# RWKV attention with a mixture of experts: the bonus term as column-half matmuls, one step order for all chunks, zero-padded tiles, four routing groups

## The chip, the cores and the metric

The kernel runs on one core of one Trainium2 chip. The metric is the device time of one execution in microseconds, as the median of three runs: 420.6 us before the change (420.49 to 426.0).

## The reference

The inputs r, k, v are 4 batches x 8 heads x 768 positions x 48, in fp32. Attention first, a linear recurrence for each batch and head, with a decay w and a bonus u for each head and channel:

```python
for t in range(S):
    cur = np.einsum('bhd,bhe->bhde', u[None] * kt, vt)
    y[:, :, t] = np.einsum('bhd,bhde->bhe', rt, state + cur)
    state = w[None, :, :, None] * state + np.einsum('bhd,bhe->bhde', kt, vt)
```

Its result, as 3072 tokens x 384, goes through a mixture of 8 experts (384 to 1024 to 384) in which each token uses one expert:

```python
e_idx = np.argmax(x @ w_gate, axis=1)
probs = softmax(x @ w_gate)                 # gate_w: probs at e_idx
eom = 1.0 / (1.0 + np.exp(-(x @ w_output_gate)))
h = np.maximum(x[mask] @ w1[e], 0.0)
out[mask] = gate_w[mask, None] * eom[mask, e, None] * (h @ w2[e])
```

The bonus part of a row of y is v times one number for each token and head, the sum over d of r·u·k.

## The kernel before

**Attention in chunks.** The 3072 tokens are 24 chunks of 128 (six to a batch), and the 8 heads four pairs, each pair on the 128 partitions as two halves of 64 rows. Rn and Kn are r and k times powers of the decay (`prep`, two VectorE products, L217); `trans` turns them into RT and KT on TensorE (L264), copied out by ScalarE (L265). `scores` (L277) multiplies KT and RT into two PSUM tiles ps_a; `causal` (L281) masks them into two tiles A on VectorE. `inter` (L315) adds the state T's share of y, `intra` (L323) the chunk's own, both in PSUM (ps_y). `state` (L293) makes the new state; VectorE adds the old one (L301) and GpSimd applies the decay (L302). The bonus: `uterm` makes ku = k·u·r by two GpSimd products (L239, L240) with u_b, a 192 KB copy of u on all partitions; `bonus` sums it over each head on VectorE (coef, L249) and multiplies v by it on GpSimd (vc, L251). `output` adds ps_y and vc on VectorE into x (L330) and stores it to x_d in DRAM (L335).

**Loads.** `load(i)` issues three DMAs of 192 KB on the sync engine's queue, in the order k, r, v (L193), into pools of four buffers each; chunks 0 to 3 have buffers of their own.

**Routing.** For each chunk, x is transposed (`logits_t`, L372, L374) and multiplied by both gates' weights, 16 columns (`logits_mm`, L382). The chunks form GROUPS; a group's `group` (L394 to L610), a generator, finds each token's expert and its place in the list of that expert, by VectorE instructions on small tiles and a few matmuls, and adds two columns (token number and weight) to a table. The table's matmul runs in bf16 with five columns: the token number in two parts, the weight in three (`parts`, `rest`, `columns`, `collect`). When all but the last group are in, the most filled expert is known and its weights are loaded; the first EARLY tiles of its tokens are gathered and its first matmuls are done during the last chunks (`early_x` L793, `early_mm`).

**The order.** All five engines run in the order in which the program is written (`manual_schedule`); nothing reorders them. For each chunk i the main loop walks through the list STEP (STEP0 for chunk 0): `sc` scores, `a0`, `a1` masks, `in` inter, `xt` transposes of x(i−1), `tr` transposes of chunk i+1, `p0`, `p1` Rn and Kn of chunk i+2, `ld` load(i+3), `bo` bonus, `i0`, `i1` intra, `st` state, `lm` logits of chunk i−1; x follows behind the list. At each `m` a few pending VectorE instructions of a group are put in, paid by the credit that BUDGETS gives from a chunk on (nominal costs in us); at each `t1` there is room for a group's matmul. So the place of a name in STEP is its place on each engine it uses, the sync engine's queue included.

After the chunks the expert phase runs: gather, transposes, three matmuls per product (the fp32 values are split in two), scale, scatter to the output.

Of the kernel before, what the change touches and what calls it, by code (L numbers as in the profile page):

```python
# [147 lines left out]
def make_powers(tc, pool, k, halfway):  # L148
# [34 lines left out]
def load_rkv(tc, pin, spare, srcs, b, c, first, after=None):  # L183
    nc = tc.nc
    ts = []
    for nm, s in zip("krv", (srcs[1], srcs[0], srcs[2])):
        if nm in first:
            t = first[nm][:, :, :D]
        elif spare:
            t = spare.pop(0).rearrange("p (h d) -> p h d", h=H)  # L190
        else:
            t = pin.tile([C, H, D], F32, name=f"{nm}_t")
        nc.sync.dma_start(t, s[b, :, c * C : (c + 1) * C, :].rearrange("h p d -> p h d"))  # L193
        ts.append(t)
        if after and nm == "k":
            after()
    return [ts[1], ts[0], ts[2]]


class Attention:  # L200
    def __init__(self, tc, ctx, k, load, x_d):
# [31 lines left out]
    def uterm(self, i):  # L233
        if i >= NT:
            return
        nc, k = self.tc.nc, self.k
        rt, kt, vt = self.load(i)
        ku = self.pw.tile([C, H, D], F32, name="ku")
        nc.gpsimd.tensor_mul(ku, kt, k.u_b.rearrange("p (h d) -> p h d", h=H))  # L239
        nc.gpsimd.tensor_mul(ku, ku, rt)  # L240
        self.ku[i] = ku

    def bonus(self, i):
        if i >= NT:
            return
        nc = self.tc.nc
        vt = self.load(i)[2]
        coef = self.pw.tile([C, H], F32, name="coef")
        nc.vector.tensor_reduce(out=coef, in_=self.ku.pop(i), axis=AX.X, op=ALU.add)  # L249
        vc = self.pw.tile([C, H, D], F32, name="vc")  # L250
        nc.gpsimd.tensor_mul(vc, vt, coef.unsqueeze(2).to_broadcast((C, H, D)))  # L251
        self.vc[i] = vc
# [86 lines left out]
class Router:  # L339
    def __init__(self, tc, pool, k, wg, wog):  # L340
        nc = tc.nc
        self.tc, self.k = tc, k
        self.wg32 = pool.tile([C, KC, 2 * E], F32, name="wg32")
        nc.sync.dma_start(self.wg32[:, :, :E], wg.rearrange("(c p) e -> p c e", p=C))
        nc.sync.dma_start(self.wg32[:, :, E:], wog.rearrange("(c p) e -> p c e", p=C))
# [31 lines left out]
    def logits_mm(self, ps, xT, tag="u"):  # L377
        pl = ps.tile([C, 512], F32, name="ps_l", tag=tag, bufs=1)
        for j in range(KC):
            for c in range(2):  # L380
# [1 line left out]
                self.tc.nc.tensor.matmul(pl[half, : 2 * E], xT[:, j, half], self.wg32[:, j, :], start=(j == 0), stop=(j == KC - 1), skip_group_check=True)  # L382
# [11 lines left out]
    def group(self, ps, w, lg, i0, G, closing, last):  # L394
# [41 lines left out]
        def weighting():  # L436
# [20 lines left out]
            rest = scale  # L457
            for i in range(3):
                nc.vector.tensor_copy(parts[:, i], rest)
                yield  # L460
                if i < 2:
                    nxt = mk(f"rest{i}")
                    nc.vector.tensor_sub(nxt, rest, parts[:, i])
                    rest = nxt
                    yield

        parts = None if last else w.tile([C, 3, G], BF16, name=f"parts_{G}", tag="parts")
# [5 lines left out]
        nc.tensor.matmul(cnt, k.tri, oh16.rearrange("p c e -> p (c e)"), start=True, stop=(G == 1 and (first or based)), skip_group_check=True)  # L473
        if not first and not based:
            nc.tensor.matmul(cnt, k.ones16, rep(self.csum16), start=False, stop=(G == 1), skip_group_check=True)
        for c in range(G - 1):
            nc.tensor.matmul(cnt[:, (c + 1) * E :], k.ones16, oh16[:, c, :].unsqueeze(1).to_broadcast((C, G - 1 - c, E)), start=False, stop=(c == G - 2), skip_group_check=True)
# [33 lines left out]
        sel = hold("sel", W, dt=BF16)  # L511
# [7 lines left out]
        ohp = hold("ohp", QP, dt=BF16)  # L519
# [3 lines left out]
        rhs = hold("rhs", 5, W, dt=BF16)  # L523
        (nc.vector if last else nc.gpsimd).tensor_mul(rhs[:, :, 0], sel, bc(k.tile0[:, cols], W))
        nc.scalar.activation(rhs[:, :, 1], sel, AF.Copy, scale=k.row1)
        tab = self.tab

        def columns(i):
            nc.vector.tensor_mul(rhs[:, :, 2 + i], sel, bc(parts[:, i], W))
# [15 lines left out]
        if last:  # L545
            yield P
            pt = product(0, 2)
            for i in range(2):
                yield V
                collect(pt, i)  # L550
# [26 lines left out]
            pt = product(2, 5)
            for i in range(2, 5):
                yield V
                collect(pt, i)  # L580
# [21 lines left out]
        collect(pt, 4)
# [13 lines left out]

    def order(self, ps, w):
# [3 lines left out]
        nc.tensor.matmul(pt[:, :E], k.ones, self.csum, start=True, stop=True)  # L621
# [782 lines left out]
```

## Time and profile before

| | |
|---|---|
| median of 3 runs | 420.6 us (420.49 to 426.0) |
| the profiled execution's own time | 422.5 us |
| its span in the profile | 420.8 us |
| TensorE busy | 372.9 us, 89% of the span |
| VectorE busy | 256.6 us, 61% |
| ScalarE busy | 152.1 us, 36% |
| GpSimd busy | 165.5 us, 39% |
| x(0), x(21), x(23) end at | 17.16, 151.46, 167.58 us |
| moved by DMA | 55.01 MB, mean 131 GB/s |

In the profile's rows PE is TensorE (PEld its weight loads), DVE VectorE, ACT ScalarE, POOL GpSimd, and SP the sync engine, SPq its DMA queue; L and a number is the line of the kernel. "out<-in" are the tiles written and read. Text in square brackets is how long the engine stood idle before the row, and what it waited for. The attention chunks fill the first 168 us of the span, the experts the rest.

### The profile page before, as it was taken

How to read it: one execution, taken by the hardware profiler on the slowest of the kernel's cores; microseconds unless marked ns; L12 is line 12 of the kernel's file. 1: busy time of each engine (PE TensorE's matmuls, PEld its weight loads, DVE VectorE, ACT ScalarE, POOL GpSimd, SP SyncE). 2: the span in 40 equal slices, each digit the busy share in tenths (PEclk: the TensorE clock that was granted, in tenths of full speed). 3: DMA queues.
4: the chain of work that ended last, by engine and by line, in shares of the span. 5: the costliest groups of instructions: out<-in, count | busy, mean ns of one | idle time of the engine just before them, and what ended most of it. 6: DMA issues, size and time to landing. Idle time of an engine off the chain costs nothing. (4 is left out here: it accounts for less than half of the span.)

```text
span 420.8 us, 11171 instructions
## 1 busy us (share of the span) xinstructions
PE 372.9 (89%) x4500; PEld 352.2 (84%) x4500; DVE 256.6 (61%) x592; ACT 152.1 (36%) x310; POOL 165.5 (39%) x215
## 2 busy tenths in 40 slices
PE   7799789878967696995998999999999999999990
PEld 4688678777867695995997999999999999999980
DVE  5878898989988963552875266266363663636300
ACT  2223232223232332421455265264453553625210
POOL 6967456555556644524041032222313503301010
PEclk8899899989979866896999999999999999999996
DMA  8957566646686611045528165174273552830010
GB/s 135 174 130 162 106 149 142 141 104 134 142 213 176 153 58 58 20 134 168 151 66 280 38 210 169 43 239 157 65 241 129 185 191 88 261 122 34 2 43 18
DMA packets 104696, 55.01 MB, mean 131 GB/s; under 512 B 78511, under 2 KB 102243, under 8 KB 104624
## 3 DMA queue, kind: packets, MB, share of 16 engines
q1 hardware_dynamic: 101200, 44.27, 41.2%
q0 software_dynamic: 3424, 9.82, 6.9%
q8 instruction: 40, 0.66, 0.6%
q14 instruction: 32, 0.26, 0.2%
HBM read 44.64 MB, written 9.76 MB: 129 GB/s over the span
## 5 line engine op out<-in xcount | busy, mean ns | idle before, releaser
L847 POOL DMA_INDIRECT out_dram<-yo,si x28 | 28.7, 1026 | 134.1 <-ACT yo L844 72.7
L810 PE MATMUL ps_h<-xh,w1h 128*128 128x384 f32 (+4 forms) x216 | 74.7, 346 | 6.0 <-issue 4.7
L811 PE MATMUL ps_h<-xl,w1h 128*128 128x384 f32 (+4 forms) x216 | 72.5, 336 | 0.0
L812 PE MATMUL ps_h<-xh,w1l 128*128 128x384 f32 (+4 forms) x216 | 72.4, 335 | 0.0
L781 POOL DMA_INDIRECT xg<-x_d,gi x28 | 31.2, 1115 | 46.0 <-PE ps_xt L793 31.1
L810 PEld LDWEIGHTS ps_h<-xh,w1h 128*128 128x128 f32 x216 | 42.6, 197 | 7.4 <-issue 5.0
L820 DVE SCALAR_TENSOR_TENSOR hl<-ps_h,hh 128x384 fp32r<-128x384 f32 (+4 forms) x72 | 38.0, 533 | 17.2 <-ACT hh L819 16.8
L819 ACT ACTIVATE hh<-ps_h 128x384 fp32r<-128x384 f32 (+4 forms) x72 | 33.7, 472 | 32.7 <-PE ps_h L812 32.7
L374 ACT COPY xT<-ps_x 128x384 f32<-128x384 f32 x24 | 11.5, 479 | 91.7 <-PE ps_x L372 83.6
L872 PE MATMUL ps_o<-w2h,hh 128*128 128x384 f32 x128 | 43.5, 340 | 0.0
L873 PE MATMUL ps_o<-w2l,hh 128*128 128x384 f32 x128 | 42.9, 335 | 0.0
L811 PEld LDWEIGHTS ps_h<-xl,w1h 128*128 128x128 f32 x216 | 42.7, 198 | 0.1
L874 PE MATMUL ps_o<-w2h,hl 128*128 128x384 f32 x128 | 42.8, 334 | 0.0
L812 PEld LDWEIGHTS ps_h<-xh,w1l 128*128 128x128 f32 x216 | 42.6, 197 | 0.2
L759 DVE TENSOR_TENSOR w1l<-raw,w1h 128x768 fp32r<-128x768 f32 x28 | 26.7, 955 | 23.4 <-ACT w1h L758 21.0
L758 ACT CAST w1h<-raw 128x768 fp32r<-128x768 f32 (+1 forms) x36 | 27.1, 764 | 27.0 <-PE ps_h L811 19.9
L281 DVE TENSOR_TENSOR A<-ps_a,mask 128x512 f32<-128x512 f32 x48 | 31.3, 683 | 5.7 <-PE ps_a L277 5.7
L796 DVE TENSOR_TENSOR xl<-ps_xt,xh 128x384 fp32r<-128x384 f32 (+4 forms) x27 | 13.9, 538 | 32.4 <-ACT xh L795 32.1
L251 POOL TENSOR_TENSOR vc<-v_t,coef 128x384 f32<-128x384 f32 x21 | 21.3, 1014 | 28.0 <-DVE coef L249 18.1
L759 DVE TENSOR_TENSOR w2l<-raw,w2h 128x768 fp32r<-128x768 f32 x28 | 26.7, 958 | 7.4 <-ACT w2h L758 5.7
L758 ACT CAST w2h<-raw 128x768 fp32r<-128x768 f32 (+1 forms) x36 | 26.7, 765 | 8.4 <-PE ps_o L874 4.4
L323 PE MATMUL ps_y<-v_t,A 128*64 128x48 f32 x672 | 29.3, 237 | 0.0
(224 smaller groups left out, 784.4 us busy)
## 6 DMA issues: line engine op xcount, KB each, us to landing
raw<-in_moe_w_dram SPq DMA_DIRECT2D x64, 384.0 KB, 3.5
x_d<-x SPq DMA_DIRECT2D x24, 192.0 KB, 1.9
v_t<-in_v_dram SPq DMA_DIRECT2D x21, 192.0 KB, 4.7
k_t<-in_k_dram SPq DMA_DIRECT2D x20, 192.0 KB, 3.0
r_t<-in_r_dram SPq DMA_DIRECT2D x20, 192.0 KB
raw<-in_v_dram SPq DMA_DIRECT2D x3, 192.0 KB
raw<-in_k_dram SPq DMA_DIRECT2D x3, 192.0 KB
xg<-x_d,gi POOLq DMA_INDIRECT x28, 4.7
```

The lines of the kernel that those rows point to most:

```text
L281: self.tc.nc.vector.tensor_mul(a, self.pa[j], self.k.mask.unsqueeze(1).to_broadcast((C, NP, C)))
L758: nc.scalar.copy(hi, self.raw[i][:, cs])
L759: (eng or nc.vector).tensor_sub(lo, self.raw[i][:, cs], hi)
L781: nc.gpsimd.indirect_dma_start(out=self.xg[q][:n], out_offset=None, in_=self.x_d[:n_x, :], in_offset=bass.IndirectOffsetOnAxis(ap=self.rt. ...
L810: nc.tensor.matmul(o, wh[:, j, fs], xh, start=(j == 0), stop=False)
L811: nc.tensor.matmul(o, wh[:, j, fs], xl, start=False, stop=False)
L812: nc.tensor.matmul(o, wl[:, j, fs], xh, start=False, stop=(j == KC - 1))
L819: nc.scalar.activation(hh, o, AF.Relu)
L820: nc.vector.scalar_tensor_tensor(hl, o, 0.0, hh, op0=ALU.max, op1=ALU.subtract)
L872: nc.tensor.matmul(o, hh, wh, start=(f == 0), stop=False)
L873: nc.tensor.matmul(o, hh, wl, start=False, stop=False)
L874: nc.tensor.matmul(o, hl, wh, start=False, stop=(f == FC - 1))
```

## The change

The bonus coefficient is made on TensorE: GpSimd multiplies RT and KT into P (`product`), eight matmuls, one for each head pair and half of the tokens, multiply P by a small matrix uw (u over the decay, zero-padded) into ps_b, and one VectorE product multiplies v by the two columns of ps_b that belong to a pair (`values`). ku, coef, the GpSimd vc and u_b go. Scores and inter use all 64 rows of a half instead of 48, and the gate weights are padded from 16 to 48 columns. STEP and STEP0 are written anew: `pr` is product, `vc` values, `x` the output, which now has its place in the list; `ld` stands behind `x`, and `p1` behind both; there are four `m` instead of six. The routing groups are four instead of five, and their table has two fp32 columns in place of five in bf16; its matmuls and the counting ones are cut into two column halves.

```diff
-GROUPS = [(0, 5), (5, 5), (10, 4), (14, 4), (18, 6)]
+GROUPS = [(0, 7), (7, 7), (14, 4), (18, 6)]
+HALVES = (slice(0, HB), slice(HB, C))
-STEP = ['m', 'sc', 'a0', 'm', 'a1', 'in', 'xt', 't1', 'm', 'tr', 't1', 'ld', 'ut', 'bo', 'm', 'p0', 'm', 'p1', 'lm', 'i0', 'st', 'i1', 'm']
+STEP = ['sc', 'a0', 'a1', 'in', 'm', 'tr', 'xt', 'p0', 'm', 'bo', 'vc', 't1', 'st', 'pr', 'i0', 'i1', 'lm', 't1', 'm', 'x', 'ld', 'p1', 'm']
-BUDGETS = [[0, 0.25], [16, 0.3]]
+BUDGETS = [[0, 0.25], [14, 0.3], [18, 0.45]]
-STEP0 = ['sc', 'a0', 'm', 'a1', 'in', 'tr', 'ld', 'bo', 'm', 'p0', 'm', 'p1', 'i0', 'st', 'i1', 'm']
+STEP0 = ['sc', 'a0', 'a1', 'tr', 'in', 'p0', 'bo', 'vc', 'st', 'pr', 'i0', 'i1', 'x', 'ld', 'p1']
...
-    def uterm(self, i):
...
-        nc.gpsimd.tensor_mul(ku, kt, k.u_b.rearrange("p (h d) -> p h d", h=H))
-        nc.gpsimd.tensor_mul(ku, ku, rt)
...
-        nc.vector.tensor_reduce(out=coef, in_=self.ku.pop(i), axis=AX.X, op=ALU.add)
-        vc = self.pw.tile([C, H, D], F32, name="vc")
-        nc.gpsimd.tensor_mul(vc, vt, coef.unsqueeze(2).to_broadcast((C, H, D)))
+    def product(self, i):
...
+        self.P = self.pw.tile([C, NP, C], F32, name="P", bufs=1)
+        self.tc.nc.gpsimd.tensor_mul(self.P, RT, KT)
+
+    def bonus(self, ps):
+        pb = self.pb = ps.tile([C, 512], F32, name="ps_b", tag="at", bufs=2)
+        for q in range(NP):
+            for half in HALVES:
+                self.tc.nc.tensor.matmul(pb[half, D * q : D * (q + 1)], self.P[:, q, half], self.k.uw[:, q, :], start=True, stop=True)
+
+    def values(self, i):
+        coef = self.pb[:, : NP * D].rearrange("p (q c) -> p q c", q=NP)[:, :, :2]
+        vc = self.pw.tile([C, H, D], F32, name="vc", bufs=1)
+        split = lambda t: t.rearrange("p (q j) d -> p q j d", j=2)
+        self.tc.nc.vector.tensor_mul(split(vc), split(self.st[i][2]), coef.unsqueeze(3).to_broadcast((C, NP, 2, D)))
...
-                rows = slice(HB * j, HB * j + D)
+                rows = HALVES[j]
...
-        self.wg32 = pool.tile([C, KC, 2 * E], F32, name="wg32")
+        self.wg32 = pool.tile([C, KC, D], F32, name="wg32")
+        nc.gpsimd.memset(self.wg32[:, :, 2 * E :], 0.0)
...
-        sel = hold("sel", W, dt=BF16)
+        sel = hold("sel", W)
-        ohp = hold("ohp", QP, dt=BF16)
+        ohp = hold("ohp", QP)
-        rhs = hold("rhs", 5, W, dt=BF16)
+        rhs = hold("rhs", 2, W)
...
             for c in range(G):
-                nc.tensor.matmul(pt[:, lo * W : hi * W], ohp[:, c, :], rhs[:, c, lo:hi].rearrange("p a w -> p (a w)"), start=(c == 0), stop=(c == G - 1), skip_group_check=True)
+                for hf in HALVES:
+                    nc.tensor.matmul(pt[hf, lo * W : hi * W], ohp[:, c, hf], rhs[:, c, lo:hi].rearrange("p a w -> p (a w)"), start=(c == 0), stop=(c == G - 1), skip_group_check=True)
...
-        load(1, lambda: nc.sync.dma_start(u_b, u.rearrange("h d -> (h d)").unsqueeze(0).to_broadcast((C, DM))))
+        k.ut = load_heads(tc, const, u, "ut", 0.0)
+        load(1)
...
+                        elif a == "x":
+                            X[i] = att.output(i)
...
-                    x = att.output(i)
```

The change moves rows on three engines at places that matter below. First the sync engine's queue at the end of chunks 0 and 1, before and then after; raw_71, xg_110 and the first v_t are the buffers of k, r and v of chunk 3, the k_t, r_t and next v_t those of chunk 4.

```order
18 L193 DMA raw_71<-in_k_dram 128x8x48
19 L193 DMA xg_110<-in_r_dram 128x8x48
20 L193 DMA v_t<-in_v_dram 128x8x48
21 L335 DMA x_d<-x 128x384
22 L193 DMA k_t<-in_k_dram 128x8x48
23 L193 DMA r_t<-in_r_dram 128x8x48
24 L193 DMA v_t<-in_v_dram 128x8x48
25 L335 DMA x_d<-x 128x384
```

```order
18 L339 DMA x_d<-x 128x384
19 L200 DMA raw_71<-in_k_dram 128x8x48
20 L200 DMA xg_110<-in_r_dram 128x8x48
21 L200 DMA v_t<-in_v_dram 128x8x48
22 L339 DMA x_d<-x 128x384
23 L200 DMA k_t<-in_k_dram 128x8x48
24 L200 DMA r_t<-in_r_dram 128x8x48
25 L200 DMA v_t<-in_v_dram 128x8x48
```

Each chunk's loads have moved behind the store of one more x: those of chunk 3 stood ahead of the store of x(0) and now stand behind it, and so on to the last chunk.

Then VectorE in chunk 2, before and after; the second number of a name counts its buffers, A is the masked score tile, and the r_t and k_t that it reads here are those of chunk 4.

```order
46 L281 TENSOR_TENSOR A_561<-ps_a_543,mask 128x512
47 L281 TENSOR_TENSOR A_563<-ps_a_544,mask 128x512
48 L249 TENSOR_REDUCE coef<-ku 128x8
49 L217 TENSOR_TENSOR Rn_297<-r_t,PR 128x8x48
50 L217 TENSOR_TENSOR Kn_300<-k_t,PK 128x8x48
51 L301 TENSOR_TENSOR T_643<-ps_u,T 128x192
52 L330 TENSOR_TENSOR x<-ps_y,vc 128x384
```

```order
47 L285 TENSOR_TENSOR A_572<-ps_a_554,mask 128x512
48 L285 TENSOR_TENSOR A_574<-ps_a_555,mask 128x512
49 L222 TENSOR_TENSOR Rn_304<-r_t,PR 128x8x48
50 L255 TENSOR_TENSOR vc<-raw_71,ps_b 128x384
51 L305 TENSOR_TENSOR T_635<-ps_u,T 128x192
52 L334 TENSOR_TENSOR x<-ps_y,vc 128x384
53 L222 TENSOR_TENSOR Kn_307<-k_t,PK 128x8x48
```

The reduction has gone, the product vc stands behind Rn and ahead of T and x, and Kn has moved behind x. The r_t that Rn reads here was issued two stores of x earlier before, and one store earlier now.

Last TensorE, the second half of chunk 1 and the first scores of chunk 2, before and after; ps_y is the output, ps_u the state's update, ps_t the transposes, ps_x the transposed x of chunk 0, ps_l its logits, ps_b the bonus columns. "64x128" and "128x128" are a matmul's output.

```order
45 L315 MATMUL ps_y<-T,RT 64x48 x16
46 L372 MATMUL ps_x<-ident,x 128x128 x3
47 L264 MATMUL ps_t<-ident,Kn_301 128x128 x4
48 L264 MATMUL ps_t<-ident,Rn_297 128x128 x4
49 L382 MATMUL ps_l<-wg_151,xT 64x16 x6
50 L323 MATMUL ps_y<-raw_69,A_446 64x48 x8
51 L293 MATMUL ps_u<-raw_69,Kn_300 64x48 x8
52 L323 MATMUL ps_y<-raw_69,A_448 64x48 x8
53 L277 MATMUL ps_a_543<-RT,KT 64x128 x2
```

```order
46 L319 MATMUL ps_y<-T,RT 64x48 x16
47 L268 MATMUL ps_t<-ident,Kn_308 128x128 x4
48 L268 MATMUL ps_t<-ident,Rn_304 128x128 x4
49 L377 MATMUL ps_x<-ident,x 128x128 x3
50 L249 MATMUL ps_b<-uw,P 64x48 x8
51 L297 MATMUL ps_u<-raw_69,Kn_307 64x48 x8
52 L327 MATMUL ps_y<-raw_69,A_451 64x48 x8
53 L327 MATMUL ps_y<-raw_69,A_453 64x48 x8
54 L387 MATMUL ps_l<-wg_153,xT 64x48 x6
55 L281 MATMUL ps_a_554<-RT,KT 64x128 x2
```

The bonus matmuls have come in, the transposes of x stand behind those of Kn and Rn, the state ahead of intra and the logits at the end. In both orders the form changes three times in a chunk: 48-row inputs (scores, inter) to full 128x128 transposes to 64-row outputs and back.

More of the change, by code (lines that the diff above doesn't have):

```diff
@@ L171, in make_powers @@
     k.pr, k.pk, k.w128 = pr, pk, sq[7]
+    k.uw = pool.tile([C, NP, D], F32, name="uw")
+    nc.gpsimd.memset(k.uw, 0.0)
+    for j in range(2):
+        rows = slice(HB * j, HB * (j + 1))
+        nc.gpsimd.tensor_mul(k.uw[rows, :, j], k.ut[rows], sq[0][rows])
 def make_tables(tc, pspool, k):
@@ L180, in make_tables, with load_rkv @@
         nc.scalar.copy(dst, ps[:, :, :D])
-def load_rkv(tc, pin, spare, srcs, b, c, first, after=None):
+def load_rkv(tc, pin, spare, srcs, b, c, first):
     nc = tc.nc
@@ L456, in weighting @@
             yield
[L457 to L467, printed above, removed]
         side = iter(()) if last else weighting()
@@ L472, in group @@
         based = last
[L473 to L477, printed above, removed]
+        halves = (slice(0, C),) if last else HALVES
+        for hf in halves:
+            nc.tensor.matmul(cnt[hf], k.tri[:, hf], oh16.rearrange("p c e -> p (c e)"), start=True, stop=(G == 1 and (first or based)), skip_group_check=True)
+            if not first and not based:
+                nc.tensor.matmul(cnt[hf], k.ones16[:, hf], rep(self.csum16), start=False, stop=(G == 1), skip_group_check=True)
+            for c in range(G - 1):
+                nc.tensor.matmul(cnt[hf, (c + 1) * E :], k.ones16[:, hf], oh16[:, c, :].unsqueeze(1).to_broadcast((C, G - 1 - c, E)), start=False, stop=(c == G - 2), skip_group_check=True)
         next(side, None)
@@ L522, in group, with weights @@
         yield Slot(0.3)
-        rhs = hold("rhs", 5, W, dt=BF16)
-        (nc.vector if last else nc.gpsimd).tensor_mul(rhs[:, :, 0], sel, bc(k.tile0[:, cols], W))
-        nc.scalar.activation(rhs[:, :, 1], sel, AF.Copy, scale=k.row1)
+        rhs = hold("rhs", 2, W)
+        (nc.vector if last else nc.gpsimd).tensor_mul(rhs[:, :, 0], sel, bc(k.id1[:, cols], W))
         tab = self.tab
-        def columns(i):
-            nc.vector.tensor_mul(rhs[:, :, 2 + i], sel, bc(parts[:, i], W))
+        def weights():
+            nc.vector.tensor_mul(rhs[:, :, 1], sel, bc(self.scale[:, cols], W))
         def product(lo, hi):
@@ L546, in group @@
             yield P
[L547 to L550, printed above, removed]
+            pt = product(0, 1)
+            yield V
+            collect(pt, 0)
             yield V
@@ L569, in group @@
             yield SPLIT
-            parts = w.tile([C, 3, G], BF16, name=f"parts_{G}", tag="parts")
             for _ in weighting():
                 yield V
-            for i in range(3):
-                columns(i)
-                yield V
+            weights()
             yield P
[L577 to L580, printed above, removed]
+            pt = product(1, 2)
+            yield V
+            collect(pt, 1)
             yield V
@@ L589, in group @@
             yield V
-        for i in range(3):
-            yield Slot(0.2)
-            columns(i)
+        yield Slot(0.2)
+        weights()
         yield P
-        pt = product(0, 5)
+        pt = product(0, 2)
         if closing:
-            self.early(pt[:, 5 * W :])
-        for a, b in ((0, 2), (1, 3)):
+            self.early(pt[:, 2 * W :])
+        for a in range(2):
             yield V
             collect(pt, a)
-            collect(pt, b)
-        yield V
-        collect(pt, 4)
         if closing:
@@ L620, in order @@
         pt = ps.tile([C, 512], F32, name="ps_ord", tag="g", bufs=1)
-        nc.tensor.matmul(pt[:, :E], k.ones, self.csum, start=True, stop=True)
+        for hf in HALVES:
+            nc.tensor.matmul(pt[hf, :E], k.ones[:, hf], self.csum, start=True, stop=True)
         yield V
@@ L1159, in rwkv_top1_moe, with load @@
         ready, pin = {}, []
-        def load(i, after=None):
+        def load(i):
             if i < NT and i not in ready:
-                ready[i] = load_rkv(tc, pin and pin[0], spare, (r, kk, v), *divmod(i, NCH), k.raw0 if i == 0 else {}, after)
+                ready[i] = load_rkv(tc, pin and pin[0], spare, (r, kk, v), *divmod(i, NCH), k.raw0 if i == 0 else {})
             return ready.get(i)
@@ L1278, in rwkv_top1_moe @@
                     att.prep(*a)
[L1279 to L1281 removed]
+                att.product(0)
+                X = {}
                 for i in range(NT):
```

80 lines of the change are left out of this document (32 added, 48 removed).

## The prediction, made before the changed kernel ran

> **What bounds the kernel now.** I read the busy times by stage first. x(n) is the attention output of chunk n, and its VectorE row (L330) marks the chunk's end. The rows shown run from the end of x(0) (17.16) to those of x(21) and x(23), to the steady expert phase and to the end. A row gives the stretch, its length, busy time (and instructions) of PE, PEld, DVE, ACT and POOL, granted clock, DMA share and GB/s.
>
> ```profile
> 17.16:151.46 134.30, 112.71 (x2708) 102.31 (x2712) 117.03 (x292) 40.23 (x104) 81.77 (x91) 0.91 0.63 142
> 151.46:167.58 16.12, 12.86 (x254) 11.30 (x246) 7.91 (x25) 4.07 (x11) 7.03 (x8) 0.71 0.24 75
> 167.58:196.00 28.42, 23.54 (x168) 22.71 (x169) 12.21 (x50) 8.31 (x23) 12.34 (x13) 0.86 0.32 100
> 196.00:420.80 224.80, 211.98 (x1235) 207.74 (x1233) 107.86 (x189) 95.75 (x166) 51.23 (x48) 0.98 0.41 130
> ```
>
> After 196 us TensorE is busy 94% of the time with expert matmuls that the change leaves alone. The 134.30 us from x(0) to x(21) are what it works on: 21 chunks, 6.4 us each, TensorE busy 84%, VectorE 87%. So neither alone sets the pace. A chunk without routing-group work shows which does when it is undisturbed (timeline: start, duration, engine, line):
>
> ```profile
> 63.92 1.10 PE L277 MATMUL ps_a<-RT,KT 48*64 48x128 f32 x32
> 65.81 0.55 PE L372 MATMUL ps_x<-ident,x 128*128 128x128 f32 x3 [0.33 <-DVE A L281]
> 67.16 0.53 PE L382 MATMUL ps_l<-wg,xT 128*64 128x16 f32 x12
> 67.53 0.65 PE L323 MATMUL ps_y<-v_t,A 128*64 128x48 f32 x16
> 68.03 0.67 PE L293 MATMUL ps_u<-v_t,Kn 128*64 128x48 f32 x16
> 68.53 0.64 PE L323 MATMUL ps_y<-v_t,A 128*64 128x48 f32 x16
> 69.10 0.89 PE L277 MATMUL ps_a<-RT,KT 48*64 48x128 f32 x24
> 64.04 0.56 DVE L330 TENSOR_TENSOR x<-ps_y,vc 128x384 f32<-128x384 f32 x1
> 65.06 1.29 DVE L281 TENSOR_TENSOR A<-ps_a,mask 128x512 f32<-128x512 f32 x2 [0.46 <-PE ps_a L277]
> 66.27 0.54 DVE L249 TENSOR_REDUCE coef<-ku 128x8 f32<-128x384 f32 x1
> 66.73 0.55 DVE L217 TENSOR_TENSOR Rn<-r_t,PR 128x384 f32<-128x384 f32 x1
> 67.19 1.18 DVE L217 TENSOR_TENSOR Kn<-k_t,PK 128x384 f32<-128x384 f32 x1
> 68.82 0.36 DVE L301 TENSOR_TENSOR T<-ps_u,T 128x192 f32<-128x192 f32 x1 [0.45 <-PE ps_u L293]
> 69.22 0.56 DVE L330 TENSOR_TENSOR x<-ps_y,vc 128x384 f32<-128x384 f32 x1
> ```
>
> Scores start at 63.92 and again at 69.10: 5.18 us, TensorE-bound but for its wait of 0.33 on the mask. 21 such chunks are 109 us; the other 25 of the 134 are what the routing groups push in, mostly on VectorE.
>
> **Where the next loads stand.** This decides the forecast. The sync queue in the same chunk, the landing of its k load (last line of the loads' answer, 64 to 71 us), and what DMA moved (the last column is GB/s):
>
> ```profile
> 64.63 0.36 SPq L335 DMA_DIRECT2D x_d<-x  x1
> 65.04 0.42 SPq L193 DMA_DIRECT2D k_t<-in_k_dram  x1
> 65.50 0.70 SPq L193 DMA_DIRECT2D r_t<-in_r_dram  x1
> 66.32 0.54 SPq L193 DMA_DIRECT2D v_t<-in_v_dram  x1
> DMA to landing us min/median/max: 3.2/3.2/3.2
> 66.20:67.20 1.00, 1.00 (x12) 0.83 (x10) 1.00 (x4) 0.75 (x2) 0.74 (x2) 1.00 0.92 177
> 67.20:68.20 1.00, 1.00 (x35) 1.00 (x34) 1.00 (x2) 0.78 (x3) 0.76 (x1) 1.00 0.97 195
> 68.20:69.20 1.00, 1.00 (x36) 0.95 (x38) 0.54 (x2) 0.00 (x0) 0.00 (x0) 1.00 1.05 209
> 69.20:69.80 0.60, 0.60 (x24) 0.60 (x28) 0.56 (x1) 0.00 (x0) 0.54 (x2) 1.00 0.20 53
> ```
>
> The queue runs in order, so k, r and v leave behind the store of x: x ends at 64.60, k is issued at 65.04, r at 65.50. k lands 3.2 us after its issue, at 68.24. Then r: the three loads of 192 KB end by about 69.4, at some 195 GB/s or 1 us apiece. I put r 0.8 us behind k, at 69.04, which is **4.4 us after x ends**. The bounds are 3.6 (together with k) and 4.8 (with the last byte). Before, the loads behind x(n) are for chunk n+4 and nothing on TensorE or VectorE waits for them. After, they are for chunk n+3, and their first user, the Rn product of chunk n+3, is a VectorE row of chunk n+1, between its mask products and its vc, T and x. A stall there holds all three, and x(n+1) releases the next loads.
>
> On this the Trainium skill, page "DMA: Bandwidth & Descriptors", section "Rules for kernel authors", says to issue a transfer early and wait on it late. The change does the reverse; by that rule alone the chunk grows by whatever latency is not covered. The trace agrees insofar as only GpSimd shows a wait for these loads before.
>
> **The new loop, x(n) to x(n+1).** Landing of r 4.4; Rn to the next row 0.46 (66.73 to 67.19); vc the same 0.46, since it is a 128x384 product out of PSUM like x (0.56 busy); T 0.36; x 0.56. Sum 6.24 us, against 5.18 for TensorE. The loop repeats 21 times: 131.0. In three of them (last chunk of a batch) T is absent, −1.1: **129.9**.
>
> **The edits by part.** The coefficient reduction (0.54) goes and the product vc (0.56) comes on VectorE: nothing. GpSimd loses ku and its vc and gains P:
>
> ```profile
> L251 POOL TENSOR_TENSOR vc<-v_t,coef 128x384 f32<-128x384 f32 x21 | 21.3, 1014 | 28.0 <-DVE coef L249 18.1
> ```
>
> Three such instructions of 1.0 us become one of 512 elements, by size 1.35; it starts when the transposes are copied and is wanted a chunk later, so it is hidden, and if it weren't it would cost at most its 1.35 per chunk. TensorE gains the bonus matmuls, 16 records in 128x64 like those of L323 (67.53 to 68.03): 0.50. Its chunk, without the wait for the mask, becomes 4.85 + 0.50 = 5.35 at most, inside the loop. Wider logits cost nothing: 12 records of width 16 took 0.37 (67.16 to 67.53), 16 of width 48 took 0.50, both 31 ns each. 64 rows in place of 48 are one record each as before. If the loop didn't cover TensorE, these would cost 0.5 per chunk.
>
> The mode order hides nothing large either. The step from the last L323 to the scores took 0.57 where the one within the mode took 0.50: 0.07 per change of mode, three per chunk before and, counted in the order, three after. The Trainium skill ("TensorEngine Tiling (Array Packing)", "Key Properties") says a mode change drains the array; with half the group matmuls freed of such changes the sum would fall by under 2 us, and TensorE waits in that time anyway.
>
> **Routing work inside the loop.** VectorE groups by line, 17.2 to 151.4 us (count | busy us, mean ns):
>
> ```profile
> L281 DVE TENSOR_TENSOR A<-ps_a,mask 128x512 f32<-128x512 f32 x42 | 27.4, 682 | 4.0 <-PE ps_a L277 4.0
> L217 DVE TENSOR_TENSOR Kn<-k_t,PK 128x384 f32<-128x384 f32 x20 | 17.3, 864 | 0.0
> L217 DVE TENSOR_TENSOR Rn<-r_t,PR 128x384 f32<-128x384 f32 x20 | 13.3, 663 | 0.0
> L330 DVE TENSOR_TENSOR x<-ps_y,vc 128x384 f32<-128x384 f32 x21 | 11.6, 550 | 1.3 <-PE ps_y L323 0.6 <-POOL w1l L759 0.6
> L249 DVE TENSOR_REDUCE coef<-ku 128x8 f32<-128x384 f32 x21 | 11.4, 543 | 0.0
> L529 DVE TENSOR_TENSOR rhs<-sel,parts 128x160 bf16<-128x160 bf16 (+1 forms) x12 | 6.7, 571 | 0.0
> L301 DVE TENSOR_TENSOR T<-ps_u,T 128x192 f32<-128x192 f32 x15 | 5.3, 354 | 7.3 <-PE ps_u L293 6.4 <-PE ps_y L323 0.9
> L459 DVE CAST parts<-rest 128x5 bf16<-128x5 f32 (+1 forms) x8 | 4.6, 576 | 0.0
> ```
>
> The six rows of chunk work are 86 of the 117 us, so about 30 are group work. It loses the parts (4.6, and some 2 in smaller rows), two thirds of the rhs columns (4.5), one of five groups and most collects (3); wider fp32 tiles give back an estimated 1. About 16 stay. Of the four places for it in a chunk, two (behind the masks, behind Kn) lie in the wait for r or before the scores, two (behind Rn, behind T) in the loop: half, **8 us**, between 5 and 10. The first expert's weights join the queue around chunks 18 to 20 (by the order, one to three at a time behind a chunk's loads):
>
> ```profile
> raw<-in_moe_w_dram SPq DMA_DIRECT2D x64, 384.0 KB, 3.5
> ```
>
> Two take 4 us at 195 GB/s, behind v's end at 4.8, so the last reaches some 2.5 us into the next loop of 6.24 and delays its r by an estimated 1 us, in two chunks: **+2**, between 0 and 4. That gives 129.9 + 8 + 2 = 140 against 134.3: **+5.7**.
>
> **The two ends.** At the start VectorE waits for GpSimd's ku; at the end TensorE waits for the gathered rows and then runs slowly:
>
> ```profile
> 13.99 0.55 DVE L249 TENSOR_REDUCE coef<-ku 128x8 f32<-128x384 f32 x1 [0.82 <-POOL ku L240]
> 163.21 1.83 PE L793 MATMUL ps_xt<-ident,xg 128*128 128x128 f32 x6 [2.97 <-DMA xg<-x_d,gi]
> 161.50:171.70 10.20, 8.46 (x70) 7.81 (x71) 1.83 (x4) 4.71 (x12) 5.27 (x6) 0.50 0.13 42
> ```
>
> Without ku, chunk 0 saves that wait, one reduction and the moved Kn, **−2** (0 to −2.5). Chunks 22 and 23 load nothing that is waited for: two TensorE chunks and a little, 10.7 instead of 16.1, if the closing group's indices come in time, **−5.4** (0 to −6). Then the half clock (0.50) on the first expert matmuls goes as well, of 4.1 us behind 167.58 about half: **−2**; wider last tables **+0.5**.
>
> **Sum.** 5.7 − 2 − 5.4 − 2 + 0.5 = −3.2 us. The profiled execution took 422.5 us by its own time, with a span of 420.8 us; 419.3 by that. The median of the three runs is 420.6, so 417.4 by that: I say **418**, no change that counts.
>
> **Rivals.** (A) *r comes in time.* If it lands under 3.5 us after x, the loop is under 5.35 and TensorE bounds the chunk: 21 × 5.35 = 112 us, with half of the 25 us of group stalls left some 124, so 16 less than my 140: **402**. For it: the lower bound 3.6 lies close. Against: k alone took 3.6 from x's end, and r is issued behind it. 20%. (B) *The loop is longer, and the end is slower.* One mechanism: r lands with the last byte or queues behind other traffic. Each 0.1 us is 2.1 us of time; from 4.95 us on the kernel is over 2% slower, and at 5.05 it takes 418 + 13.7 = **432**. For it: the transfers already run at 0.9 to 1.05 of the DMA engines. Against: before, the last byte of the same loads comes 4.8 us after x. 16%. (C) *The clock drops.* TensorE now idles about 1 us a chunk (6.24 − 5.35). At half clock a chunk's 5.35 us become 10.7 against 6.24, and 21 of them add 94 us: 512. The trace shows 0.50 behind a wait of 2.97 us, not behind waits below 1. 2%. The Trainium skill ("TensorE: Matmul & The Clock Gate", "What's actually happening") puts the drop behind an idle window of about 3.4 us, which fits that row; gaps of 1 us would keep the clock. (D) *The change doesn't do what it says at the end:* the closing indices come late as before, +5: **423**, inside no change; 10%, taken out of the forecast's 62% in all.
>
> **Chances.** Forecast and D 62%, A 20%, B 16%, C 2%. About 2%, 8.4 us, is what a measurement of this kernel can tell from no change. A and a slice of the forecast (r at 4.1 or less) are faster: 0.25; B and C slower: 0.18; 0.57 remain. Of the unknowns r's landing weighs most: 3.75 to 5.0 us in place of 4.4 give 404 to 431, which takes in the bounds of the smaller terms and leaves out C and half each of A and B.
>
> **What would show it.** Right: VectorE waits before Rn for r's DMA in nearly each chunk, about 1 us; x follows x in 6.2 us in chunks without group work; TensorE waits about 1 us per chunk, its clock near 1; the wait for xg at the end is gone. Wrong: the Rn row without a wait and 5.3 us per chunk (A), or 6.8 and more (B); vc or P late on TensorE's or GpSimd's account, for which I leave nothing.

## The result, and the profile after

The changed kernel takes **439.7 us** (438.5 to 440.8) against 423.3 for the kernel before over the same runs: a ratio of 1.038 (95% interval 1.028 to 1.049), slower. The forecast was no change at 418, with a range of 404 to 431. Times are medians of all runs, and ratios leave out the runs that were over 1.5% longer than the fastest of their kernel. The profiled execution took 438.5 us, its span is 436.6.

Busy times by stage of the changed kernel, cut at the ends of x(0), x(6), x(18), x(21) and x(23); the columns are those of the table shown of before:

```profile
16.22:56.29 40.07, 32.33 (x841) 29.82 (x834) 21.71 (x42) 9.60 (x23) 10.44 (x10) 0.96 0.56 120
56.29:145.13 88.84, 71.98 (x1819) 65.62 (x1814) 54.01 (x136) 20.67 (x54) 20.43 (x21) 0.94 0.54 118
145.13:173.89 28.76, 21.74 (x509) 19.20 (x509) 24.03 (x61) 8.75 (x22) 13.96 (x14) 0.88 0.61 153
173.89:184.08 10.19, 9.72 (x256) 8.92 (x257) 6.97 (x18) 4.21 (x12) 7.80 (x8) 1.00 0.41 119
184.08:436.60 252.52, 234.24 (x1435) 228.60 (x1433) 118.88 (x228) 103.41 (x187) 63.42 (x60) 0.97 0.40 127
```

From x(0) to x(21) it takes 157.67 us, where the kernel before took 134.30: 23.4 more, though VectorE is now busy for 100 of these us instead of 117. Something is waited for, and the first row shows it free of routing work: chunks 1 to 6 hold none, and still take 40.07 / 6 = 6.68 us each, with TensorE busy 81% and VectorE 54%. The list of waits names it (total us, times, longest):

```profile
DVE Rn L222 <- DMA r_t<-in_r_dram: 38.9, 18, 2.9
```

One chunk without routing work, from x(11) to x(12):

```profile
94.20 0.55 DVE L334 TENSOR_TENSOR x<-ps_y,vc 128x384 f32<-128x384 f32 x1
...
94.78 0.36 SPq L339 DMA_DIRECT2D x_d<-x  x1
95.13 1.29 DVE L285 TENSOR_TENSOR A<-ps_a,mask 128x512 f32<-128x512 f32 x2
...
95.67 0.69 SPq L200 DMA_DIRECT2D r_t<-in_r_dram  x1
...
99.22 0.56 DVE L222 TENSOR_TENSOR Rn<-r_t,PR 128x384 f32<-128x384 f32 x1 [2.80 <-DMA r_t<-in_r_dram]
99.70 0.55 DVE L255 TENSOR_TENSOR vc<-v_t,ps_b 128x384 f32<-128x384 f32 x1
100.16 0.35 DVE L302 TENSOR_TENSOR T<-ps_u,sq 128x192 f32<-128x192 f32 x1
100.43 0.55 DVE L334 TENSOR_TENSOR x<-ps_y,vc 128x384 f32<-128x384 f32 x1
100.66 0.56 PE L387 MATMUL ps_l<-wg,xT 128*64 128x48 f32 x12 [1.96 <-DVE T L302]
...
101.00 0.36 SPq L339 DMA_DIRECT2D x_d<-x  x1
```

This is the loop of the forecast: x ends at 94.75, its store and behind it r are issued, Rn starts 4.47 us after x, and vc, T and x follow. TensorE waits as well: its logits stand behind T (they use the PSUM tile that T reads), the next scores behind vc (which reads ps_b, and ps_b and ps_a share their two buffers). The chunk takes 6.22 us; 6.24 was forecast. So the mechanism was foreseen and its price in this chunk is right. What was wrong is how far this chunk speaks for the others.

### The profile page after: what moved, and what is told of

Same layout as the page of the kernel before. It is cut to its first block, busy times and chain, and to the rows that moved or that the text cites. A ratio compares the mean times of both kernels' runs of the same rounds, so it can differ in the third digit from the quotient of the medians.

```text
span 436.6 us, 12118 instructions
## 1 busy us (share of the span) xinstructions
PE 383.4 (88%) x4996; PEld 362.1 (83%) x4996; DVE 235.9 (54%) x516; ACT 150.3 (34%) x303; POOL 125.4 (29%) x170
## 3 DMA queue, kind: packets, MB, share of 16 engines
q1 hardware_dynamic: 101472, 44.08, 38.9%
## 5 line engine op out<-in xcount | busy, mean ns | idle before, releaser
L799 PE MATMUL ps_h<-xh,w1h 128*128 128x384 f32 (+4 forms) x216 | 73.4, 340 | 4.1 <-issue 4.1
L800 PE MATMUL ps_h<-xl,w1h 128*128 128x384 f32 (+4 forms) x216 | 71.5, 331 | 0.0
L770 POOL DMA_INDIRECT xg<-x_d,gi x28 | 31.2, 1116 | 45.0 <-PE ps_xt L782 29.5
L800 PEld LDWEIGHTS ps_h<-xl,w1h 128*128 128x128 f32 x216 | 41.6, 192 | 0.1
L801 PEld LDWEIGHTS ps_h<-xh,w1l 128*128 128x128 f32 x216 | 41.4, 192 | 0.2
L243 POOL TENSOR_TENSOR P<-RT,KT 128x512 f32<-128x512 f32 x24 | 32.6, 1360 | 23.1 <-ACT xT L379 17.7
L747 ACT CAST w1h<-raw 128x768 fp32r<-128x768 f32 (+1 forms) x36 | 27.1, 763 | 26.6 <-PE ps_h L800 22.9
L306 POOL TENSOR_TENSOR T<-T,sq 128x192 f32<-128x192 f32 x16 | 8.1, 506 | 87.2 <-DVE T L305 82.1
L281 PE MATMUL ps_a<-RT,KT 64*64 64x128 f32 x768 | 31.1, 299 | 2.0 <-DVE vc L255 2.0
L222 DVE TENSOR_TENSOR Rn<-r_t,PR 128x384 f32<-128x384 f32 x20 | 11.7, 587 | 38.9 <-DMA r_t<-in_r_dram 38.9
L269 ACT COPY KT<-ps_t 128x512 f32<-128x512 f32 x23 | 13.5, 586 | 54.3 <-PE ps_t L268 54.3
L387 PE MATMUL ps_l<-wg,xT 128*64 128x48 f32 x288 | 13.2, 225 | 20.4 <-DVE T L305 9.5
```

What stands on the lines that cost most here:

```text
L243: self.tc.nc.gpsimd.tensor_mul(self.P, RT, KT)
L281: nc.tensor.matmul(self.pa[j][half, q, :], KT[rows, q, half], RT[rows, q, :], start=True, stop=True)
L770: nc.gpsimd.indirect_dma_start(out=self.xg[q][:n], out_offset=None, in_=self.x_d[:n_x, :], in_offset=bass.IndirectOffsetOnAxis(ap=self.rt. ...
L799: nc.tensor.matmul(o, wh[:, j, fs], xh, start=(j == 0), stop=False)
L800: nc.tensor.matmul(o, wh[:, j, fs], xl, start=False, stop=False)
L801: nc.tensor.matmul(o, wl[:, j, fs], xh, start=False, stop=(j == KC - 1))
```

## The experiments

Each number beside a time is the ratio to the kernel before, run beside it, with its interval; the changed kernel has 1.038.

**1. The loads issued a store earlier.** In the changed kernel:

```diff
-STEP = ['sc', 'a0', ... 'm', 'x', 'ld', 'p1', 'm']
+STEP = ['ld', 'sc', 'a0', ... 'm', 'x', 'p1', 'm']
```

and the same in STEP0.

> The changed kernel with 'ld' at the head of STEP and STEP0 instead of behind 'x': the loads of chunk n+4 again leave right behind the store of x(n), as before the change, and nothing else moves. Theory L (late loads): the changed kernel's chunk is the loop store of x, landing of r, Rn, vc, T, x. Then VectorE's wait before Rn for r (38.9 us in 18 chunks) goes to nearly nothing, chunks without group work fall from 6.0-7.3 to 5.3-5.6 us, x(0) to x(21) from 157.7 to 125-138 us, and the time from 439.7 to 410-420 us. Rival S (the new step order itself, VectorE or TensorE): the wait only covers other waits; it is replaced by waits on TensorE or the masks, chunks stay over 6 us, and the time stays at 432 or more.

Measured: **409.0 us**, 0.971 (0.963 to 0.980). The waits list has no row of Rn for r any more. By stage:

```profile
15.95:47.20 31.25, 30.68 (x855) 28.43 (x850) 24.37 (x43) 9.77 (x24) 9.51 (x10) 1.00 0.71 154
47.20:116.72 69.52, 65.22 (x1810) 59.75 (x1798) 55.72 (x135) 20.26 (x52) 19.84 (x21) 1.00 0.67 146
116.72:143.19 26.47, 20.64 (x509) 18.04 (x509) 23.52 (x60) 8.68 (x22) 13.34 (x14) 0.94 0.60 160
```

Chunks 1 to 6 take 5.21 us, TensorE busy 98%; from x(0) to x(21) it is 127.24 us, 30.4 less than in the changed kernel. Rival S said that something else would be waited for and nothing much would come: it falls. Moving one name in a list turns 4% slower into 3% faster.

**2. The same lateness put into the kernel before.** There 'ld' is taken out of the two lists and load(i + 3) and load_raw stand behind att.output(i); all else is as before.

> The kernel before with its loads issued behind x instead of in the middle of the list, so that they leave one store of x later, and nothing else changed. Theory L: the same loop appears in it: r lands 4.4 to 5.2 us after x, then Rn, Kn, T, x (1.9 us): 6.3 to 7.1 us a chunk where it was 5.2, less where group work already held VectorE; 11 to 21 chunks lose 1 to 1.5 us each: 434 to 446 us, with VectorE waiting for r's DMA in most chunks. Rival S: loads a store later are still hidden by the six slots' order; at most 4 us slower, 421 to 425.

Measured: **459.3 us**, 1.093 (1.084 to 1.102), slower than theory L expected. Its waits, one chunk's rows, and the stage from x(0) to x(21):

```profile
POOL ku L239 <- DMA k_t<-in_k_dram: 76.1, 20, 5.4
DVE Rn L217 <- DMA r_t<-in_r_dram: 41.7, 18, 4.1
```

```profile
38.01 0.54 DVE L330 TENSOR_TENSOR x<-ps_y,vc 128x384 f32<-128x384 f32 x1
...
42.05 1.00 POOL L239 TENSOR_TENSOR ku<-k_t,u_b 128x384 f32<-128x384 f32 x1 [3.07 <-DMA k_t<-in_k_dram]
43.18 0.56 DVE L217 TENSOR_TENSOR Rn<-r_t,PR 128x384 f32<-128x384 f32 x1 [2.97 <-DMA r_t<-in_r_dram]
43.66 1.35 DVE L217 TENSOR_TENSOR Kn<-k_t,PK 128x384 f32<-128x384 f32 x1
44.93 0.34 DVE L301 TENSOR_TENSOR T<-ps_u,T 128x192 f32<-128x192 f32 x1
45.20 0.54 DVE L330 TENSOR_TENSOR x<-ps_y,vc 128x384 f32<-128x384 f32 x1
```

```profile
17.11:188.03 170.92, 132.10 (x2728) 118.29 (x2728) 119.04 (x292) 42.28 (x104) 84.82 (x90) 0.79 0.51 115
```

The loop appears here too, and longer: Kn stands in it, and since GpSimd's ku waits for the same loads the two run together, and Kn takes 1.35 us beside it. This chunk takes 7.19 us; a chunk of before without routing work took 5.2. Unforeseen was the clock in the last row: 0.79 over the stage where it was 0.91 before. So the 9% are the longer loop and a slower TensorE, in shares that this run doesn't separate.

**3. Only r issued first.** In load_rkv the order of the three DMAs is r, k, v from chunk 3 on.

> The changed kernel with each chunk's three loads from chunk 3 on issued in the order r, k, v instead of k, r, v: r leaves 0.46 us earlier and is the first to land. Theory L: r lands 0.5 to 1.0 us earlier, each of the 18 chunks that wait for it is shorter by as much: 9 to 18 us, 422 to 431. Rival S: no change, 437 to 442.

Measured: **423.9 us**, 1.005 (0.999 to 1.011). r lands 3.9 us after x on the mean of chunks 1 to 18, 0.84 earlier than in the changed kernel; the time falls by 15.8 us, and of VectorE's wait 12.0 us are gone:

```profile
DVE Rn L224 <- DMA r_t<-in_r_dram: 26.9, 18, 2.4
```

From x(0) to x(21) it takes 142.35 us, 15.3 less than the changed kernel: each tenth of a microsecond of r's delay is worth 1.8 us (15.3 / 8.4) there; the forecast's rival B put 2.1 on it.

**4. The loads late, but Rn behind x.** 'p0' goes from behind 'xt' to behind 'p1', the loads stay where the change put them.

> The changed kernel with 'p0' (Rn of the chunk after next) moved behind 'x' and 'p1'; the loads stay behind x. Rn then has r for over a chunk and holds no vc, T and x. Theory L: the wait for r goes as in e1 although the loads are late; Rn and Kn stand together before the masks, 0.5 us on VectorE that TensorE's scores mostly cover: 5.4 to 5.9 us a chunk, 412 to 424 us. Rival S: 432 or more.

Measured: **414.7 us**, 0.983 (0.976 to 0.990). The loads leave as late as in the changed kernel, and still nothing waits for r. It isn't the late issue alone that costs, but a late issue with its user ahead of the next release.

**5 to 8, from experiment 1 on.** What else of the change counts, with the loads early.

> The changed kernel with its loads at the head of the list (as in e1_loads_first, 409.0 us) and the five routing groups of before in place of four; the new table and list stay. Theory G (fewer groups save their fixed cost): a group is some 25 small VectorE rows of 0.15 to 0.7 us, half of them between Rn and x; one more costs 3 to 6 us: 411 to 416. Rival: group rows lie in VectorE's waits for TensorE, and five are as good as four: 407 to 411.

412.2 us, 0.980 (0.975 to 0.986): 3 us more than with four groups, inside what theory G expected, but the interval overlaps that of experiment 1; inconclusive.

> As e1_loads_first, with the padding undone: gate weights of 16 columns, and 48 rows in place of 64 in scores and inter. By the prediction's step padding costs and gains nothing (31 ns a record at both widths): 407 to 411. Rival: uniform 64-row tiles let TensorE go from scores and inter to the next form faster, so that undoing them costs 0.1 to 0.3 us in each of 24 chunks: 411 to 416.

407.3 us, 0.968 (0.964 to 0.972): the padding costs and gains nothing that can be told.

> As e1_loads_first, with 'p1' (Kn) moved from behind 'x' to right behind 'p0' (Rn). In e1, Kn behind x runs beside GpSimd's P and takes 1.18 to 1.66 us instead of 0.55, and the masks of the next chunk wait for it (they start 1.1 us after x instead of 0.4 to 0.8), while behind Rn VectorE waits 0.4 to 0.7 us for the bonus matmuls. Theory K: Kn is on e1's path in some 14 chunks with 0.3 us each: 403 to 407. Rival: TensorE bounds e1's chunk, and nothing comes of it: 408 to 411.

408.6 us, 0.972 (0.967 to 0.976): nothing. Theory K falls, and the rival's forecast holds, that TensorE (busy 98% of chunks 1 to 6 in experiment 1) is the bound.

> As e7_kn_beside_rn, with the first expert's weight splits of chunks 18 to 23 (two subtractions a chunk, 2.1 to 2.3 us on GpSimd) made on VectorE instead. In e1 chunks 19, 20 and 21 take 7.7, 10.3 and 8.5 us, and small VectorE rows that take 0.2 us elsewhere take 0.7 to 1.1 beside these subtractions. Theory C (contention of GpSimd with VectorE): without it the three chunks fall by 3 to 6 us in sum, less about 1 us of VectorE time a chunk: 1 to 4 us faster than e7. Rival: TensorE, at a lower clock there (0.83), sets these chunks, and VectorE's extra work makes them longer: 0 to 4 us slower than e7.

406.9 us, 0.970 (0.964 to 0.976), not to be told from experiment 7; chunks 19 to 21 take 26.6 us together, against 25.4 in experiment 7 and 26.5 in experiment 1. The contention itself is there. One small row of chunk 20, experiment 7 first, where GpSimd makes a split beside it, then this one, where GpSimd is idle:

```profile
132.81 0.95 DVE L457 SCALAR_TENSOR_TENSOR den<-en,se 128x4 f32<-128x4 f32 x1
```

```profile
134.06 0.15 DVE L457 SCALAR_TENSOR_TENSOR den<-en,se 128x4 f32<-128x4 f32 x1
```

VectorE is busy for 23.40 us of these chunks in experiment 7 and for 22.47 here, 3.32 of them with the splits: its other rows have lost 4.25 us, and the chunks are no shorter. So VectorE's busy time alone doesn't set them. What TensorE waits for there is seen in the changed kernel itself, in chunk 19:

```profile
146.85 1.88 DVE L517 TENSOR_TENSOR ohp<-pp,ip 128x896 f32<-128x896 f32 x1
148.65 1.27 DVE L285 TENSOR_TENSOR A<-ps_a,mask 128x512 f32<-128x512 f32 x2
149.38 0.90 PE L377 MATMUL ps_x<-ident,x 128*128 128x128 f32 x3 [2.49 <-DVE A L285]
151.35 0.56 DVE L255 TENSOR_TENSOR vc<-v_t,ps_b 128x384 f32<-128x384 f32 x1 [0.66 <-PE ps_b L249]
153.33 0.36 DVE L305 TENSOR_TENSOR T<-ps_u,T 128x192 f32<-128x192 f32 x1 [1.42 <-PE ps_u L297]
```

Routing rows at the place behind Kn push the masks to 3.5 us after x (145.13), TensorE waits for them, and then VectorE's vc and T wait for what TensorE makes behind them.

**9. Routing rows moved into the wait.** In the changed kernel, with the loads late, the two places between Rn and x go ahead of Rn:

```diff
-... 'tr', 'xt', 'p0', 'm', 'bo', 'vc', 't1', 'st', 'pr', 'i0', 'i1', 'lm', 't1', 'm', 'x', ...
+... 'tr', 'xt', 'm', 'm', 'p0', 'bo', 'vc', 't1', 'st', 'pr', 'i0', 'i1', 'lm', 't1', 'x', ...
```

> The changed kernel, its loads still behind x, with the two places for routing-group rows that lie between Rn and x moved ahead of Rn, into VectorE's wait for r. The prediction's step: group rows between Rn and x lengthen the loop, rows ahead of Rn are hidden in the wait. In the changed kernel chunks 7 to 18 take 85 us against 78 at the pace of chunks 1 to 6, and chunk 7, 14 and 18 also wait there 0.9 us for the logits. If the step holds, 5 to 9 us go: 430 to 435. Rival: the group rows then delay Rn itself or the masks by as much: 437 to 442.

Measured: **432.7 us**, 1.019 (1.011 to 1.026), its interval just clear of that of the 1.038: some 8 us less by the ratios (0.020 x 420.6), with the ends of the two intervals 1 to 16. (Chunks 7 to 18 of the changed kernel take 88.84 us, not the 85 of the expectation.) Routing rows between Rn and x lengthen the loop, as the prediction's step has it.

**10. The bonus as before, the rest of the change kept.** In the kernel of experiment 1 the matmuls of bonus are left out, product makes ku and values makes coef and vc, each a chunk earlier than in the changed kernel: the VectorE reduction and the three GpSimd products are back.

> As e1_loads_first (409.0), with the bonus made as before the change: ku in two GpSimd products, coef as a VectorE reduction, vc as a GpSimd product, u_b loaded; list, groups, table and padding stay. By the prediction's step the bonus alone is worth nothing on VectorE (0.54 for 0.56) and costs TensorE 0.5 a chunk, and GpSimd's 3.6 us a chunk would be hidden: where TensorE bounds e1's chunk this kernel is up to 0.5 us x 13 chunks = 6 us faster: 402 to 409. Rival B: GpSimd's three products slow VectorE's Rn and Kn and hold the start (ku): 3 to 10 us slower, 412 to 419.

Measured: **404.8 us**, 0.954 (0.948 to 0.959), clear of experiment 1. With the loads early TensorE bounds the chunk and the bonus matmuls stand in it. The starts of the scores of two chunks in a row, from x(12) on, show by how much, experiment 1 first, then this one:

```profile
81.27 1.10 PE L281 MATMUL ps_a<-RT,KT 64*64 64x128 f32 x32
84.10 0.67 PE L249 MATMUL ps_b<-uw,P 128*64 128x48 f32 x16
86.45 0.78 PE L281 MATMUL ps_a<-RT,KT 64*64 64x128 f32 x20
```

```profile
79.82 1.10 PE L280 MATMUL ps_a<-RT,KT 64*64 64x128 f32 x32
84.54 0.67 PE L280 MATMUL ps_a<-RT,KT 64*64 64x128 f32 x16
```

5.18 against 4.72 us: 0.46 us, the 0.5 of the forecast. This is the fastest version of all. The matmul bonus costs; what is left of the change here, the order with early loads, the four groups, the table and the padding, is together 4.6% faster than the kernel before. Of these only the groups and the padding were taken back alone (experiments 5 and 6); order and table were not told apart.

**11 and 12, towards a better order.**

> As e7_kn_beside_rn (408.6: loads at the head, Kn behind Rn), with the place for group rows ahead of x moved up to behind vc, so that no group row waits for the chunk's logits ahead of x. In e7 chunks 7, 14 and 18 take 6.5 to 6.7 us, 1.2 to 1.5 more than the clean ones. If that wait is the cause, 3 to 4 us go: 404 to 406. Rival: the time moves to the next chunk's masks: 407 to 410.

409.7 us, 0.967 (0.960 to 0.974): nothing; the rival's time holds. In the profiled run, the longest of the four, chunks 7, 14 and 18 do fall, to 5.2, 5.2 and 5.4 us, but chunks 19 to 21 take 31.3 us where experiment 7 has 25.4: the work has moved there.

> As e11, with 0.38 instead of 0.45 of credit for group rows at each place from chunk 18 on. In e1 and e7 chunks 19 to 21 take 25 to 27 us against 15 to 16 for clean ones, the masks start 2 to 3.5 us after x because group rows stand ahead of them, and TensorE waits up to 2.5 us for the masks. If it is the rows ahead of the masks, fewer of them a chunk spread the same work: 1 to 3 us faster than e11. Rival: all of that work has to be done before the early gather anyway, and it only moves to chunk 22: within 1 us of e11, or slower if the gather comes late.

409.8 us, 0.965 (0.958 to 0.971): within 1 us of experiment 11; the rival's time holds here too, and chunks 19 to 21 take 29.5 us. That the routing work has to be somewhere ahead of the early gather is the rival's reason; nothing here tests it by itself.

## Why the prediction was wrong

**The loop: right.** Late loads, Rn behind them, vc, T and x behind Rn. Experiments 1 to 4 show it from four sides: the wait goes when the loads leave earlier or when Rn stands elsewhere, it comes when the loads of the kernel before are made late, and it scales with r's place in the queue. Only the sign that I gave for it was too small: the waits before Rn are 2.2 us on average (38.9 / 18), where I wrote about 1.

**The landing of r: mis-sized, the first step that failed.** I took 4.4 us from one chunk, and gave 4.8, the last byte in that same chunk, as its upper bound. Over chunks 1 to 18 of the changed kernel r lands 4.14 to 5.46 us after x, on average 4.75. In nine of them it is 4.1 to 4.8 (mean 4.4, as forecast), in the other nine 4.5 to 5.5 (mean 5.1). What goes with the two sorts is told in the last section. Behind the landing the chain took 1.76 us, not 1.84. The loop is so 6.5 us, and 21 of them are 136.7 against my 129.9, some 7 us more; about 1 of it is the T that I took off in three chunks, where the chain still took 1.67 us or more. That 4.4 suits nine chunks is luck of the chunk I chose: a single chunk's row gave a value but no bounds. That landings spread could be read in the kernel before, in the same answer on the loads for the whole span, where k's landing goes to 4.7, and I quoted the one chunk instead:

```profile
DMA to landing us min/median/max: 2.7/3.0/4.7
```

**Routing work in the loop: mis-sized, the second step that failed.** I put 8 us on it and 2 on the weights' traffic. Chunks 7 to 18 take 88.84 us against 12 x 6.5 = 78, 11 more, and chunks 19 to 21 take 28.76 against 19.5, 9 more: 20 us. The weights' 2 are not seen: in chunks 19 to 21 r lands 4.3 to 5.1 us after x, as elsewhere. Nearly all of the 20 lies behind Rn. About 12 us are routing rows that stand between Rn and x, 5 of them in chunks 19 to 21. About 7 are VectorE's waits between Rn and x, for TensorE or for the logits that ScalarE copies from it; for these I had left nothing. So 12 and 7 stand where the forecast has 8, and experiment 9 gains some 8 by moving the rows.

**"Two places lie in the wait": right for Rn, not for TensorE.** Rows ahead of Rn hardly delay Rn itself, which starts 4.65 to 5.12 us after x even in chunks 19 to 21. But in chunks 19 and 20 so many of them stand ahead of the masks that these start 3.5 us after x; the wait for r is gone there (in chunk 21 it is 1.05 us), and VectorE waits 3.4 us in the two chunks for TensorE, which runs late behind the masks. Chunk 20 shows both kinds, the wait and then ten routing rows between T and x:

```profile
162.06 0.36 DVE L305 TENSOR_TENSOR T<-ps_u,T 128x192 f32<-128x192 f32 x1 [0.50 <-PE ps_u L297]
...
163.04 1.23 DVE L439 TENSOR_SCALAR eidx<-m 128x4 f32<-128x4 f32 x1
...
164.55 0.54 DVE L334 TENSOR_TENSOR x<-ps_y,vc 128x384 f32<-128x384 f32 x1
```

How much of the 9 us of these three chunks belongs to the rows' number, how much to their slowness beside GpSimd and how much to TensorE's clock (0.82 and 0.83 in chunks 19 and 20) stays open.

**The sum, term by term.** From x(0) to x(21) +23.4 where I had +5.7. The start −0.9 (x(0) ends at 16.22 instead of 17.16; forecast −2). From x(21) to x(23) 10.19 instead of 16.12, −5.9 (forecast −5.4): the gather is in time, rival D was not needed, and the clock there is 1.00. Behind it −0.7 (forecast −1.5). The total, +15.8, is the difference of the two spans.

**The rivals.** B, the longer loop, had the right side, with its point of 4.95 us; r's mean of 4.75 alone would have stayed within 2%, and the routing work did the rest. That these two errors add on the same side was not in the range, which moved r alone. C came in small part: the granted clock is 0.94 to 0.96 up to x(18) and 0.88 in chunks 19 to 21. I had read half clock off one wait of 2.97 us; the last section shows it beside waits of 1.7 to 2.4. A's chunk came true as soon as the loads were early (5.21 us for its 5.35).

**The edits at no cost.** The padding cost nothing that could be told (experiment 6). GpSimd's products and VectorE's exchange of coef for vc weren't tried alone; with all of the old bonus back, experiment 10 is faster. That the bonus matmuls were free only under the cover of the loop, and cost 0.5 us a chunk without it, is what experiment 10 shows.

## What to carry to other kernels

When a transfer is issued behind the result of a step, ask which step its first user stands in and whether that user is ahead of the next release: if so, issue, landing and the chain behind them are a loop, and its sum, not any engine's busy time, is the pace. The size of such a loop needs the spread of the landing over many steps, since its price is multiplied by all of them. An edit that is free under a wait should be priced again without that wait before it is kept.

## What the runs showed of the hardware

The two sorts of chunks differ by one small transfer. From x(10) on (end 87.62) the changed kernel's DMA shows this; the first two rows are tenths of busy time and GB/s in 40 slices of 87.6 to 93 us, then the instruction queue (packets, MB, share), two of the issues (us to landing), and the issue of r on the sync engine's queue (start, duration):

```profile
DMA  0000002999854679999721000000396799999677
GB/s 0 0 0 0 0 0 80 440 341 216 262 168 84 107 134 176 230 229 203 142 46 17 11 11 11 23 20 17 84 151 119 159 235 253 253 238 191 124 122 146
q8 instruction: 1, 0.02, 2.0%
x_d<-x SPq DMA_DIRECT2D x1, 192.0 KB, 4.0
r_t<-in_r_dram SPq DMA_DIRECT2D x1, 192.0 KB, 4.5
88.53 2.21 SPq L200 DMA_DIRECT2D r_t<-in_r_dram  x1
```

One packet of 16 KB on an instruction queue starts at 88.59 and takes 1.71 us. Then, from about 90.4 to 91.4, traffic falls to 11 to 23 GB/s, with one packet at a time in flight; only then does the store of x land, after 4.0 us, and the traffic rises again with k and r. From x(11) on, without such a packet between x and r's landing, the store lands after 2.0 us, r 3.5 us after its issue, and the issue itself takes 0.69 us instead of 2.21:

```profile
x_d<-x SPq DMA_DIRECT2D x1, 192.0 KB, 2.0
r_t<-in_r_dram SPq DMA_DIRECT2D x1, 192.0 KB, 3.5
```

Over the 18 chunks the trace has such a packet start within 3 us behind x in just the nine with the mean of 5.1. The split comes back in two other traces: in experiment 3, r lands 4.5 us after x on average in the eight chunks with such a packet and 3.5 in the other ten; in experiment 2, 5.3 in five and 4.6 in thirteen. My reading is that the packet holds up one of the 16 DMA engines, and that the store, k and r, each spread over all of them, wait for that one. This rests on the traces alone; no experiment changed the instruction traffic.

The second surprise is the clock of experiment 2, 0.79 from x(0) to x(21) where the changed kernel has 0.88 to 0.96, although TensorE is idle for 23% and 20% of that time. In both, the granted clock (the share of its full speed that TensorE is given) is either 1.00 or 0.50 in a stretch. The changed kernel first, a stretch of half clock, and the wait of TensorE just before it; then two stretches of experiment 2, and the waits at their start:

```profile
80.86:84.27 3.41, 3.41 (x65) 3.32 (x56) 1.29 (x2) 0.27 (x1) 1.58 (x2) 0.50 0.80 176
79.94 0.56 PE L387 MATMUL ps_l<-wg,xT 128*64 128x48 f32 x12 [2.35 <-DVE T L305]
```

```profile
45.79:59.43 13.64, 12.11 (x161) 11.12 (x163) 8.80 (x24) 3.98 (x10) 5.16 (x6) 0.50 0.54 117
46.22 1.10 PE L315 MATMUL ps_y<-T,RT 48*64 48x48 f32 x32 [2.18 <-POOL T L302]
86.75:107.22 20.47, 18.72 (x260) 16.62 (x260) 12.85 (x34) 5.78 (x14) 9.09 (x10) 0.50 0.52 108
85.37 0.68 PE L315 MATMUL ps_y<-T,RT 48*64 48x48 f32 x32 [1.94 <-POOL T L302]
```

The changed kernel has four such stretches of 3.4 us in chunks 3 to 13, beside waits of 1.66 to 2.35 us, and the kernel before has them beside waits of 1.68 and 1.98 us. So a wait of 2 us can go with half clock; the one wait of 5.6 us in experiment 2 lies elsewhere, at 154 us, and doesn't explain its two long stretches. Behind the waits shown, none within these is longer than 1.11 us. Why the clock stays at half for 13.6 and 20.5 us there, and for 3.4 us in the changed kernel, is open.
